# Chunked attention and a two-layer feed-forward block on one core: another planned order, copies of q on ScalarE, and weights of 14 groups turned by TensorE

## The chip, the core and the metric

The kernel runs on one core of a Trainium2 chip. The core has five engines, each with its own in-order list of instructions: TensorE (PE, matrix products into PSUM; its weight loads, PEld, overlap the products), VectorE (DVE), ScalarE (ACT), GpSimd (POOL) and SyncE (SP, which here only issues DMAs). They meet through semaphores. Sixteen DMA engines move data; a DMA is issued by an instruction on SP, on ScalarE or on GpSimd, and lands some microseconds later.

The metric is the device time of one execution in microseconds (us). The kernel before took 283.0, 283.0 and 281.61 us in three runs, median 283.0. The profile is of one more execution, which took 283.97 us; its span, from the first to the last instruction of the program, is 282.2 us.

## The reference

Attention inside chunks of 64 rows, over 8 batches, 8 heads and 576 rows (9 chunks), head size 64; then two matrix products with a leaky ReLU between them over the 4608 tokens.

```python
scores = scale * np.matmul(q_c, k_c.transpose(0, 1, 2, 4, 3))   # per chunk, 64 x 64
scores = scores - np.max(scores, axis=-1, keepdims=True)
attn = np.exp(scores)
attn = attn / (np.sum(attn, axis=-1, keepdims=True) + 1e-09)
out = np.matmul(attn, v_c)
...
x = np.ascontiguousarray(attn_out.transpose(0, 2, 1, 3)).reshape(B * S, H * D)   # 4608 x 512
h = x @ w_in                       # 512 x 2048
g = np.maximum(0.01 * h, h)
return (g @ w_out).astype(np.float32)   # 2048 x 512
```

## The kernel before

**Groups.** Attention runs over 36 groups u of 128 tokens (two chunks for each of eight heads). q, k and v are loaded from fp32 in DRAM to fp16 in SBUF by DMAs that GpSimd issues (`load_one`, L289, and `load_v`, L297); a group's q or k is one DMA, or two where it lies across two batches. v is kept for two batches at a time (`VB`), and one of them is loaded again when its last reader is done.

For each group q and k must be turned, so that the head size lies on the partitions. Either TensorE turns them (`turn`, L462: four transposes into PSUM, and a copy out), or a DMA issued by SP does (`turn_dma`, L483, into the tiles `QT` and `KT`). The sets `BY_PE` say which groups go which way; everything outside them goes by DMA. The turned q is then copied in two halves into `QZ`, one of three buffers whose other places are zeros (`spread_q`, L466), so that one product with 128 rows gives the scores of two heads (`scores`, L494). For groups turned by TensorE the copy reads PSUM and is VectorE's or ScalarE's; for the others it reads `QT` and is done by GpSimd (`COPY_P`, L252).

From the scores in PSUM on a chain follows: maximum (L503) and shift (L509) on VectorE, exp (L518) on ScalarE, sum (L524) on VectorE, the small addition of 1e-9 (`ze`, L530) on GpSimd from group 4 on, reciprocal (L536) and product (L548, the weights `en`) on VectorE. The weights are turned by TensorE (`turn_e`, L557, and a copy into `et`) for the groups in `BY_PE['e']`, by a DMA from SP otherwise (L570). `values` (L582) multiplies them with v into `xp`, and ScalarE writes `xT` (L592), a ring of twelve groups.

**The two layers** run over 14 blocks of tokens (four of 128, four of 256, six of 512). The first layer's unit is `mm1` (L683): 16 products of 128, 8 of 256 or 4 of 512 columns by block, evacuated by ScalarE with the leaky ReLU (L695). In blocks named in `L1S`, four units of eight 256-column products are replaced, for each entry, by a form with seven quarter products in place of eight (`layer1`, L888 for its products), with sums before and after on VectorE. The second layer is `mm2` (L706) in the first four blocks, and the same seven-product form (`product`, L784) in the others, with forms of the weights `WF` and of the activations (L757) made by VectorE.

**The order.** The kernel does not leave the order to a scheduler. Every piece of work is a task with the engines it may run on, an occupancy and a latency in microseconds, what it depends on, and a position. `Planner.run` plays a clock: at each step it takes, on the engine that is free first, the ready task with the lowest position, chooses the engine where there is a choice, and emits the instruction at once. So the order of every engine's list, and which engine does a copy, follow from the planner's numbers: the `copy` prices, `LAG`, the model of the DMA queues in `advance` and `run` (delays and landings by kind: sw for loads by GpSimd, turn for transpositions, hw for stores), and the hand-set `HOLD`, `NUDGE` and `TWEAK`. On the chip only the lists and the semaphores count: an engine waits at its next instruction until what that needs is there. A load on GpSimd also waits until the load eight before it has landed, which is mirrored in the planner:

```python
fl = self.flight.setdefault(t.dma[0] == "sw", [])
if len(fl) >= 8 and fl[-8] not in self.done:
    continue
```

PSUM has eight banks: six (`mm`) for products and turned q and k, one for the scores (`Sp`), one for turned weights and values (`ox`). `fill` (L1091) puts products of ones into planned gaps in the first 24 us.

Of the kernel before, what the change touches and what calls it, by code (L numbers as in the profile page):

```python
# [21 lines left out]
class Planner:  # L22
# [4 lines left out]
    def __init__(self, banks, slack, margin, hold, nudge):  # L27
# [5 lines left out]
        self.hold, self.nudge = hold, nudge  # L33
        self.slack, self.margin = slack, margin
# [24 lines left out]
    def advance(self, to):  # L59
# [12 lines left out]
    def finish(self, n, end):  # L72
        self.done[n] = end
        for key, left in list(self.held.items()):
            if n in left:
                left.discard(n)
                if not left:
                    del self.held[key]
                    self.banks[key[0]][key[1]] = end
        for m in self.after.get(n, ()):  # L80
            self.need[m] -= 1
            if self.need[m] == 0:
                self.can[m] = max([self.hold.get(m, 0.0)] + [self.done[d] + self.LAG for d in self.tasks[m].deps])

    def run(self):
# [8 lines left out]
        while self.can or self.landings or any(self.queues.values()):  # L94
            best = {}
            for n, since in self.can.items():
# [41 lines left out]
            if t.dma:  # L138
                kind, work, packet = t.dma
                ahead = min(6.0, sum(x[1] for x in self.queues.get("sw", ())))  # L140
                delay = {"sw": 1.35, "turn": ahead, "hw": 0.3 + ahead, "first": 1.2 + ahead}[kind]
                if kind == "sw" and not self.flight[True]:
                    delay = 2.2
# [8 lines left out]
def kernel(  # L152
# [24 lines left out]
    G = 2 * CH  # L177
# [6 lines left out]
    SUBS = {11:512,12:512}  # L184
    L1S = {8: (1,), 10: (1,), 11: (0, 1, 2), 12: (0, 1), 13: (0, 1, 2)}
    WQAT = 0.5
# [6 lines left out]
    ATT = -0.65  # L193
    FORM = -0.86
    WFAT = 0.31
    VLAG = 5
    BY_PE = {'q': (0, 1, 2, 3, 4, 5, 6, 7, 8, 13, 18), 'k': (0, 1, 2, 3, 4, 5, 6, 7, 8), 'e': (0, 1, 2, 3, 4, 5, 6, 7, 8, 19)}
# [4 lines left out]
    HOLD = {('v', 3): 28.7, ('k', 2): 14.1, ('q', 5, 0): 31.9, ('G', 0, 2, 0): 20.9, ('n', 0): 11.9, ('k', 3): 18.8, ('c', 0): 15.1, ('e', 0): 13.3, ('tq', 4): 24.6, ('s', 2): 15.0, ('G', 2, 2, 0): 33.8, ('q', 5, 1): 29.5, ('m', 1): 11.9, ('G', 2, 3, 0): 32.8, ('tq', 0): 6.1, ('tk', 5): 30.8, ('G', 2, 0, 0): 28.7, ('m', 4): 29.4}  # L202
    NUDGE = {('M', 12, 5, 0): 0.04, ('M', 8, 1, 1): 0.11, ('M', 13, 3, 0): 0.07, ('A', 9, 3, 1): -0.07, ('M', 11, 4, 0): -0.08}
    SPREAD = 1.26
    COPY_M = ("ACT", "DVE")
    COPY_L = ("ACT",)
    FILL = 24.0
    FILLS = 0.8
    MARGIN = 0.29
    TWEAK = {(4, 12): 0.39, (0, 4): -0.39, (5, 4): -0.05, (17, 5): -0.31, (32, 1): 0.26, (33, 5): -0.04, (4, 11): -0.13, (4, 2): -0.06, (0, 9): 0.13, (25, 2): -0.59, (2, 2): 0.3, (6, 0): 0.43}  # L210
    A_LEAD = 0.18
    ORDER = (1, 6, 5, 7, 2, 4, 3)
    ORDER1 = (1, 2, 6, 5, 7, 3, 4)
# [4 lines left out]
    def sub(j):  # L218
# [19 lines left out]
        {"mm": ["qp", "kp", "mm0", "mm1", "mm2", "mm3"], "Sp": ["Sp"], "ox": ["ox"]}, SLACK, MARGIN, HOLD, NUDGE  # L238
# [82 lines left out]
    RATE = {"row": 1 / 1120, "w": 1 / 188}  # L321

    def load(name, emit, deps, count, kind):
        issue = 0.58 + 0.00028 * count
        add(("landed",) + name, {"POOL": (issue, issue)}, emit, deps, pos=-20.0 + 0.001 * len(loads),
            dma=("sw", count * RATE[kind], RATE[kind]))
# [282 lines left out]
    for u in range(NU):  # L609
        p = att  # L610
        for n, name in enumerate("qk"):
# [6 lines left out]
            else:  # L618
# [4 lines left out]
                add(("t" + name, u), {"SP": (1.3, 1.3)}, turn_dma(name, u), here, dma=("turn", 0.9, 0.0014), pos=p(u, n))  # L623
        qe = {e: copy[e] for e in (COPY_Q if u in BY_PE["q"] else COPY_P)}
# [507 lines left out]
```

## Time and profile before

| what | value |
|---|---|
| three runs | 283.0, 283.0, 281.61 us |
| profiled execution | 283.97 us |
| its span | 282.2 us |
| TensorE busy, share of the span | 272.0 us, 96% |
| VectorE | 207.8 us, 74% |
| ScalarE | 174.0 us, 62% |
| GpSimd | 136.8 us, 48% |
| mean granted TensorE clock | 0.994 |
| read from HBM, written | 36.70 MB, 9.44 MB |

How to read it: busy time is the time in which an engine runs instructions of its own; a DMA that is under way is not in it. TensorE's products overlap, so a row's duration is longer than the step from one start to the next, and prices are taken start to start. In a timeline a row is a start, a duration, an engine, a line of the kernel, an operation, what is written and read, the shape and a count of merged instructions; a bracket tells the idle time ahead of it and what ended that. In busy time by stretches a row has the stretch's bounds and length, then busy time and number of instructions of PE, PEld, DVE, ACT and POOL, the granted TensorE clock, the DMA share and GB/s. In groups of instructions a row has the busy time and the mean duration of one in ns, then the idle time in front and what ended most of it. A row of the list of waits has the total, the number and the longest.

### The profile page before, as it was taken

To read this page: it belongs to the slowest core of one execution; us is meant where nothing else is said; L and a number is where in the kernel's file an instruction comes from. 1 tells how busy PE (TensorE), PEld (TensorE's weight loads), DVE (VectorE), ACT (ScalarE), POOL (GpSimd) and SP (SyncE) were. 2 spreads that over 40 slices of the span, in tenths; PEclk is the share of its full clock that TensorE was granted. 3 is DMA by queue.
4 is the path that set the end of the run, shared out by engine and by line. 5 is a ranking of instruction groups with operands and counts; after the bars stand their busy time and mean duration, and the time that the engine had idled before them with its cause. 6 is when DMAs were issued, how large, how long until landed. Compare 5 with 4: busy or idle time off the path is not lost.

```text
span 282.2 us, 7367 instructions
## 1 busy us (share of the span) xinstructions
PE 272.0 (96%) x3008; PEld 235.2 (83%) x3008; DVE 207.8 (74%) x365; ACT 174.0 (62%) x314; POOL 136.8 (48%) x194
## 2 busy tenths in 40 slices
PE   7799999996999999999999999999999999999995
PEld 7689965784899999999989899998788788888884
DVE  7698888474767768879837967889669977583752
ACT  5347765772656477776745566755787667877421
POOL 8858675837695545474946875565323000000000
PEclk9999999997999999999999999999999999999999
DMA  8999999999999999999999999999984113100223
GB/s 141 155 186 172 181 190 156 216 124 174 128 162 159 163 143 188 177 145 150 98 125 162 138 187 197 139 203 175 140 180 104 21 38 105 65 2 0 77 82 142
DMA packets 164193, 38.75 MB, mean 137 GB/s; under 512 B 155200, under 2 KB 159808, under 8 KB 164160
## 3 DMA queue, kind: packets, MB, share of 16 engines
q0 software_dynamic: 114336, 18.09, 95.4%
q1 hardware_dynamic: 48784, 19.93, 42.0%
q8 instruction: 23, 0.38, 0.6%
q10 hardware_dynamic: 1040, 0.26, 0.4%
q14 instruction: 10, 0.08, 0.1%
HBM read 36.70 MB, written 9.44 MB: 163 GB/s over the span
## 4 chain that ended last, share of the span: by engine, by line
PE 85%; DMA 8%; POOL 4%; issue 1%; DVE 0%; POOLq 0%
PE hT L683 30%; PE mb L784 20%; PE mc L784 10%; PE lb L888 6%; PE ma L784 5%; DMA q_in<-in_q_dram 5%; DMA k_in<-in_k_dram 4%; PE lc L888 3%; PE oP L706 3%; PE Sp L494 3%; PE xp L582 2%; PE la L888 2%; POOL q_in L289 1%; POOL w_inT L306 1%; POOL VB L297 1%
## 5 line engine op out<-in xcount | busy, mean ns | idle before, releaser
L683 PE MATMUL hT<-xT,w_inT 128*128 128x256 f16 (+2 forms) x912 | 103.2, 264 | 0.3
L683 PEld LDWEIGHTS <-w_inT 128*128 128x128 f16 x912 | 77.9, 98 | 11.6 <-issue 0.6
L695 ACT ACTIVATE gT<-hT 128x512 f16<-128x512 f32 x104 | 61.5, 596 | 42.1 <-PE hT L683 41.8
L784 PEld LDWEIGHTS <-gT 128*128 128x128 f16 x512 | 49.3, 98 | 6.0
L784 PEld LDWEIGHTS <-S 128*128 128x128 f16 x384 | 37.3, 99 | 4.9
L530 POOL TENSOR_SCALAR ze<-z 128x8 f32<-128x8 f32 x32 | 9.5, 298 | 61.5 <-DVE z L524 60.0
L252 POOL COPY QZ<-QT 64x512 f16<-64x512 f16 x50 | 34.2, 683 | 8.1 <-DMA QT<-q_in 5.3
L289 POOL DMA_DIRECT2D q_in<-in_q_dram x39 | 33.9, 870 | 8.5 <-DMA q_in<-in_q_dram 2.5
L289 POOL DMA_DIRECT2D k_in<-in_k_dram x39 | 33.5, 858 | 7.0 <-DVE et L250 1.7
L784 PE MATMUL mb<-WF,gT 128*128 128x256 f16 x256 | 33.2, 273 | 0.0
L784 PE MATMUL mc<-w_outT,S 128*128 128x256 f16 x256 | 33.2, 273 | 0.0
L524 DVE TENSOR_REDUCE z<-ex 128x8 f32<-128x512 f16 x36 | 24.5, 681 | 10.9 <-ACT ex L518 10.8
L503 DVE TENSOR_REDUCE mx<-Sp 128x8 f32<-128x512 f32 x36 | 24.5, 682 | 10.5 <-PE Sp L494 10.4
L592 ACT ACTIVATE xT<-xp 128x512 f16<-128x512 f32 x36 | 21.4, 595 | 11.2 <-PE xp L582 11.0
L548 DVE TENSOR_TENSOR en<-ex,zi 128x512 f16<-128x512 f16 x36 | 26.7, 741 | 0.3
L518 ACT ACTIVATE ex<-sh 128x512 f16<-128x512 f32 x36 | 22.6, 627 | 5.0 <-DVE sh L509 4.5
L509 DVE TENSOR_TENSOR sh<-Sp,mx 128x512 f32<-128x512 f32 x36 | 24.6, 683 | 0.4
L297 POOL DMA_DIRECT2D VB<-in_v_dram x16 | 18.7, 1171 | 7.0 <-PE xp L582 4.3
L494 PE MATMUL Sp<-KT,QZ 128*128 128x64 f16 x288 | 14.3, 193 | 3.5 <-POOL QZ L252 2.8
L784 PE MATMUL mb<-WF,S 128*128 128x256 f16 x128 | 17.5, 282 | 0.0
L494 PEld LDWEIGHTS <-QZ 128*128 128x128 f16 x288 | 12.8, 98 | 4.9 <-POOL QZ L252 2.9
L888 PEld LDWEIGHTS <-wq 128*128 128x128 f16 x160 | 15.0, 98 | 2.0
(82 smaller groups left out, 392.4 us busy)
## 6 DMA issues: line engine op xcount, KB each, us to landing
out_dram<-osb SPq DMA_DIRECT2D x10, 512.0 KB, 3.9
VB<-in_v_dram POOLq DMA_DIRECT2D x16, 288.0 KB, 9.4
q_in<-in_q_dram POOLq DMA_DIRECT2D x31, 128.0 KB, 10.6
k_in<-in_k_dram POOLq DMA_DIRECT2D x31, 128.0 KB, 10.2
out_dram<-osb SPq DMA_DIRECT2D x14, 256.0 KB, 6.1
w_inT<-in_moe_w_in_dram POOLq DMA_DIRECT2D x8, 256.0 KB, 7.6
w_outT<-in_moe_w_out_dram POOLq DMA_DIRECT2D x4, 512.0 KB, 10.8
q_in<-in_q_dram POOLq DMA_DIRECT2D x8, 64.0 KB, 8.1
```

Source lines behind the costliest of these rows:

```text
L252: nc.gpsimd.tensor_copy(out=out, in_=in_)
L289: nc.gpsimd.dma_start(out=qk[name, u][a - u * G:z - u * G], in_=SRC[name][a // S, :, a % S:a % S + z - a, :].rearrange("h p d -> p h d"),)
L494: nc.tensor.matmul(out=Sp[:, i, :], lhsT=qz[:, 2 * m + g, e, :, :], rhs=kt[:, 2 * m + g, e, :], start=True, stop=True)
L503: nc.vector.tensor_reduce(out=st["mx", u], in_=st["S", u], axis=AXL.X, op=ALU.max)
L509: nc.vector.tensor_tensor(out=st["sh", u], in0=st["S", u], in1=st["mx", u].unsqueeze(2).to_broadcast((128, 8, CH)), op=ALU.subtract,)
L518: nc.scalar.activation(out=st["ex", u], in_=st["sh", u], func=AFT.Exp, bias=0.0, scale=SCL)
L524: nc.vector.tensor_reduce(out=st["z", u], in_=st["ex", u], axis=AXL.X, op=ALU.add)
L548: (nc.vector if eng == "DVE" else nc.gpsimd).tensor_tensor(out=st["en", u], in0=st["ex", u], in1=st["zi", u].unsqueeze(2).to_broadcast((12 ...
L683: nc.tensor.matmul(out=hT[:, i, :], lhsT=w_inT[:, t, fc * 128:(fc + 1) * 128], rhs=xT[:, r0 % RING // G:(r0 % RING + tb) // G, t, :], star ...
L695: nc.scalar.activation(out=gT(j)[:, nf * a:nf * a + nf, h * tb:h * tb + tb], in_=HT.pop((j, a, h)), func=AFT.Prelu, bias=0.0, scale=1.0, a ...
L784: nc.tensor.matmul(out=to, lhsT=lhs[:, fc, p * 128:(p + 1) * 128], rhs=rhs[:, fc, :], start=(opens and (p == 0 or j == LAST) and fc == 0), ...
L888: nc.tensor.matmul(out=to[:, i, :], lhsT=lhs[:, t, i * 128:(i + 1) * 128], rhs=rhs[:, :, t, :], start=(m in OPENS and i == 0 and t == 0), ...
```

## The change

It has four parts.

1. The planner's DMA model gets other numbers: the delay from an issue to the start of its transfer, the time from the end of a transfer to its landing, the shares of transfers under way together, and the cap on the queue ahead. A load also waits, in the plan, `GUARD` after the landing of the load eight before it, and from 40 us on at most four loads are planned in flight (`DEPTH`, `DEEP`). The lists that come out differ on every engine.
2. `COPY_P` is ScalarE in place of GpSimd, with a planner's price of its own for copies that read SBUF (`copy_sb`).
3. `BY_PE` is changed: q for groups 0 to 9 (before 0 to 8, 13 and 18), k for 0 to 9 (before 0 to 8), weights for 0 to 11, 14 and 15 (before 0 to 8 and 19).
4. The rest: the seven-product form of the first layer on 11 units in place of 10, 512-column units in blocks 12 and 13 in place of 11 and 12, temporaries of the second layer's form copied by ScalarE alone, those of the first layer's by either, the last part of w_out loaded ahead of group 6, the banks `Sp` and `ox` given to products when attention is done, and the tuning numbers.

```diff
-                self.landings.append((to + {"sw": 1.5, "turn": 0.32 + self.margin, "hw": 0.65, "first": 1.3}[kind], n))
+                self.landings.append((to + {"sw": 1.0, "turn": 0.75 + self.margin, "hw": 0.05, "first": 1.35}[kind], n))
...
+        if n in self.gives:
+            self.banks["mm"][self.gives[n]] = end
...
-                    if len(fl) >= 8 and fl[-8] not in self.done:
-                        continue
+                    if len(fl) >= 8:
+                        if fl[-8] not in self.done:
+                            continue
+                        if t.dma[0] == "sw" and self.done[fl[-8]] > 24.0:
+                            since = max(since, self.done[fl[-8]] + self.guard)
+                    if t.dma[0] == "sw" and len(fl) >= self.depth and self.now > self.deep:
+                        if fl[-self.depth] not in self.done:
+                            continue
...
-                ahead = min(6.0, sum(x[1] for x in self.queues.get("sw", ())))
-                delay = {"sw": 1.35, "turn": ahead, "hw": 0.3 + ahead, "first": 1.2 + ahead}[kind]
+                ahead = min(3.6, sum(x[1] for x in self.queues.get("sw", ())))
+                delay = {"sw": 2.1, "turn": ahead, "hw": 1.23 + ahead, "first": 1.2 + ahead}[kind]
...
-    SUBS = {11:512,12:512}
-    L1S = {8: (1,), 10: (1,), 11: (0, 1, 2), 12: (0, 1), 13: (0, 1, 2)}
-    LEAD = 3.61
-    LOADS = 'Q0 g1 i v0.0 g2 v0.1 Q2 g3 Q1 g4 Q3 g5 P2 P0 g7 P1 g6 P3 v1.0 g8 v1.1'
+    SUBS = {12: 512, 13: 512}
+    L1S = {8: (1,), 9: (1,), 10: (0, 1), 11: (0, 1), 12: (0, 1), 13: (0, 1, 2)}
+    LEAD = 4.12
+    LOADS = 'Q0 g1 i v0.0 g2 v0.1 Q2 g3 Q1 g4 Q3 g5 P2 P0 g7 P1 P3 g6 v1.0 g8 v1.1'
...
-    COPY_P = ("POOL",)
+    COPY_P = ("ACT",)
...
-    BY_PE = {'q': (0, 1, 2, 3, 4, 5, 6, 7, 8, 13, 18), 'k': (0, 1, 2, 3, 4, 5, 6, 7, 8), 'e': (0, 1, 2, 3, 4, 5, 6, 7, 8, 19)}
+    BY_PE = {'q': (0, 1, 2, 3, 4, 5, 6, 7, 8, 9), 'k': (0, 1, 2, 3, 4, 5, 6, 7, 8, 9), 'e': (0, 1, 2, 3, 4, 5, 6, 7, 8, 9, 10, 11, 14, 15)}
...
+    GUARD = 0.84
+    DEPTH = 4
+    DEEP = 40.0
-    COPY_M = ("ACT", "DVE")
-    COPY_L = ("ACT",)
+    COPY_M = ("ACT",)
+    COPY_L = ("ACT", "DVE")
-    MARGIN = 0.29
+    MARGIN = 2.08
...
+    plan.gives = {("b", NU - 1): "Sp", ("a", NU - 1): "ox"}
...
+    copy_sb = {"DVE": (0.29, 0.33), "ACT": (0.60, 0.68), "POOL": (0.66, 0.70)}
...
-        qe = {e: copy[e] for e in (COPY_Q if u in BY_PE["q"] else COPY_P)}
+        qe = {e: copy[e] for e in COPY_Q} if u in BY_PE["q"] else {e: copy_sb[e] for e in COPY_P}
```

`HOLD` gains three entries (tq 2, G 1 0 0 and z 3), `NUDGE` and `TWEAK` have other entries, and the positions `ATT`, `FORM`, `WFAT`, `WQAT` and `SPREAD` and the order `ORDER1` other values. The built lists have 6034 rows on TensorE (before 6018, weight loads counted), 370 on VectorE (361), 327 on ScalarE (262), 129 on GpSimd (166) and 91 on SP (99), where equal neighbours share a row on all but the first.

More of the change, by code (lines that the diff above doesn't have):

```diff
@@ L25, with __init__ @@
     LAG = 0.06
-    def __init__(self, banks, slack, margin, hold, nudge):
+    def __init__(self, banks, slack, margin, hold, nudge, guard, late, depth, deep):
         self.tasks, self.done, self.began = {}, {}, {}
@@ L33, in __init__ @@
         self.hold, self.nudge = hold, nudge
+        self.guard, self.late = guard, late
+        self.depth, self.deep = depth, deep
+        self.gives = {}
         self.slack, self.margin = slack, margin
@@ L83, in finish @@
                 self.can[m] = max([self.hold.get(m, 0.0)] + [self.done[d] + self.LAG for d in self.tasks[m].deps])
+                if self.can[m] > 30.0:
+                    self.can[m] += self.late.get(m[0], 0.0)
     def run(self):
@@ L320 @@
     loads: list[tuple] = []
-    RATE = {"row": 1 / 1120, "w": 1 / 188}
+    RATE = {"row": 1 / 1120, "w": 1 / 193}
+    PACKET = {"row": 0.00102, "w": 0.00044}
     def load(name, emit, deps, count, kind):
@@ L325, in load @@
         add(("landed",) + name, {"POOL": (issue, issue)}, emit, deps, pos=-20.0 + 0.001 * len(loads),
-            dma=("sw", count * RATE[kind], RATE[kind]))
+            dma=("sw", count * RATE[kind], PACKET[kind]))
         loads.append(name)
```

39 lines of the change are left out of this document (20 added, 19 removed).

## The prediction

> **What bounds the kernel now.** I read the page first, then busy time by stretches, then TensorE's timeline around the one weak stretch, and only then the engine that TensorE waited for there.
>
> ```profile
> span 282.2 us, 7367 instructions
> PE 272.0 (96%) x3008; PEld 235.2 (83%) x3008; DVE 207.8 (74%) x365; ACT 174.0 (62%) x314; POOL 136.8 (48%) x194
> ...
> 0.00:22.00 22.00, 17.96 (x273) 16.23 (x274) 17.52 (x43) 10.54 (x16) 15.71 (x26) 1.00 1.63 162
> 22.00:62.00 40.00, 39.94 (x518) 31.55 (x516) 30.22 (x59) 27.08 (x48) 26.43 (x34) 1.00 1.87 174
> 62.00:72.00 10.00, 7.23 (x71) 5.84 (x69) 4.65 (x8) 3.81 (x8) 6.03 (x8) 0.83 1.75 167
> 72.00:212.00 140.00, 139.99 (x1526) 124.87 (x1524) 108.66 (x185) 91.76 (x168) 85.50 (x121) 1.00 1.77 158
> ```
>
> The columns of a stretch are its bounds and length, then busy time of PE, PEld, DVE, ACT and POOL, then TensorE's granted clock. From 22 to 62 and from 72 to 212 us TensorE is busy for 179.93 of 180 us at full clock: nothing but its own list of instructions sets the time there. Only two stretches hold time that is not work: the first 22 us, and 62 to 72, where 2.77 us are idle and the clock is 0.83. TensorE's timeline shows that hole (start, duration, what; the name behind the arrow ended the wait):
>
> ```profile
> 57.94 0.39 PE L557 MATMUL tpe<-ident,en 128*128 128x128 f16 x4
> 58.16 1.91 PE L683 MATMUL hT<-xT,w_inT 128*128 128x256 f16 x16
> 59.91 0.40 PE L582 MATMUL xp<-et,VB 128*128 128x64 f16 x8
> ...
> 62.11 1.04 PE L784 MATMUL mb<-w_outT,gT 128*128 128x256 f16 x8
> 62.98 0.40 PE L582 MATMUL xp<-et,VB 128*128 128x64 f16 x8
> 66.15 0.41 PE L494 MATMUL Sp<-KT,QZ 128*128 128x64 f16 x8 [2.77 <-POOL QZ L252]
> 66.39 2.65 PE L683 MATMUL hT<-xT,w_inT 128*128 128x256 f16 x16
> 68.83 1.92 PE L784 MATMUL mb<-WF,S 128*128 128x256 f16 x8
> 70.54 1.18 PE L683 MATMUL hT<-xT,w_inT 128*128 128x256 f16 x8
> 71.56 0.40 PE L494 MATMUL Sp<-KT,QZ 128*128 128x64 f16 x8
> ```
>
> Start to start gives the undisturbed prices: sixteen hT take 59.91 - 58.16 = 1.75, eight 256-column products 62.98 - 62.11 = 0.87, four transposes 58.16 - 57.94 = 0.22, eight 64-column ones 66.39 - 66.15 = 0.24. So the scores of group 9 should have begun at 62.98 + 0.24 = 63.22 and began 2.93 late. After it sixteen hT took 2.44 (0.69 too much), eight mb 1.71 (0.84), eight hT 1.02 (0.15): the half clock that followed the hole cost 1.68. **The stall is worth 4.61 us.** The chain behind it is GpSimd's:
>
> ```profile
> 46.51 0.88 POOL L289 DMA_DIRECT2D q_in<-in_q_dram  x1 [0.96 <-DMA VB<-in_v_dram]
> ...
> 51.40 0.87 POOL L289 DMA_DIRECT2D k_in<-in_k_dram  x1 [1.04 <-PE Sp L494]
> 52.39 2.30 POOL L297 DMA_DIRECT2D VB<-in_v_dram  x2
> ...
> 62.48 0.92 POOL L289 DMA_DIRECT2D q_in<-in_q_dram  x1 [2.47 <-DMA q_in<-in_q_dram]
> 63.93 0.88 POOL L289 DMA_DIRECT2D k_in<-in_k_dram  x1 [0.53 <-DMA k_in<-in_k_dram]
> 64.81 2.63 POOL L252 COPY QZ<-QT 64x512 f16<-64x512 f16 x4
> ```
>
> ```profile
> 51.53 1.35 SPq L483 DMA_TRANSPOSE QT<-q_in  x1
> 53.00 1.40 SPq L483 DMA_TRANSPOSE KT<-k_in  x1
> ...
> QT<-q_in SPq DMA_TRANSPOSE x1, 7.2
> KT<-k_in SPq DMA_TRANSPOSE x1, 9.4
> ```
>
> The last two rows are DMA issues, with the time to landing of those two. Group 9's turned q was there at 51.53 + 7.2 = 58.7 and its k at 53.00 + 9.4 = 62.4, before TensorE asked at 63.2. The two copies of q stood behind two load issues that each waited until an earlier load had landed, and ran from 64.81 to 66.1. So a queue position was late, not the data.
>
> **The change part by part.** *The stall, -4.61.* Group 9's q and k are now turned by TensorE, and its copies run on VectorE and ScalarE. From group 10 on ScalarE copies. No copy stands behind a load issue any more. What remains on GpSimd beside loads is the 32 small additions (ze), which still wait behind load issues; in the built order the additions of groups 8 and 9 stand behind both loads of group 12.
>
> *Copies on ScalarE, 0 on the path.* There are 52 in place of 50. The trace has no ScalarE copy between fp16 tiles in SBUF; the nearest rows bound it.
>
> ```profile
> L252 POOL COPY QZ<-QT 64x512 f16<-64x512 f16 x50 | 34.2, 683 | 8.1 <-DMA QT<-q_in 5.3 <-PE Sp L494 0.8
> L248 ACT ACTIVATE QZ<-qp 64x512 f16<-64x512 f16 x12 | 7.1, 592 | 7.3 <-PE qp L462 7.1
> L916 ACT ACTIVATE gT<-lu 128x512 f16<-128x512 f32 x10 | 6.3, 630 | 3.4 <-DVE lu L911 3.3
> ```
>
> The same shape out of PSUM takes 592 ns, a read of SBUF in fp32 630; I take 610: 52 x 0.61 = 31.7 us. ScalarE goes from 174 to about 206 us (73%), and in 72 to 212 from 91.8 to about 121 of 140 (86%). It hides under TensorE as long as no evacuation of PSUM is held up; if the cover is gone, each copy ahead of an evacuation costs up to its 0.61. Beside it the temporaries of the four-product blocks go to ScalarE alone (four VectorE evictions move there), and seven of the first layer's move to VectorE. I put 0 and keep 0 to 2 us.
>
> *TensorE's list, +0.45.* Weights are turned by TensorE for 14 groups instead of 10, k for 10 instead of 9, q for 10 instead of 11: net four more sets at 0.22, +0.88. The seven-product form of the first layer runs on 11 units instead of 10: 32 hT go (2 x 1.75 = 3.50), seven products of four come (28 x 0.87 / 8 = 3.05), -0.45. Exchanging which blocks use 512 columns keeps the columns. Filler matmuls go from 160 to 156, together 0.22 us at the 56 ns of a 128-column one (0.22 / 4); those before 21.6 us only fill waits. Added: 0.88 - 0.45 = 0.43, with rounding 0.45. VectorE gains 14 instructions net, under 10 us even if each were as long as a GpSimd copy (0.683), and has 207.8 of 282.2 in use: 0 while it keeps up.
>
> *First 22 us, 0.* TensorE gets under way when the k of group 3 lands:
>
> ```profile
> 20.83 0.44 PE L1098 MATMUL idle<-ones 128*128 128x128 f16 x5
> 21.64 0.40 PE L462 MATMUL kp<-ident,k_in 128*128 128x128 f16 x4 [0.37 <-DMA k_in<-in_k_dram]
> ```
>
> The loads up to it stand in the same order, and the same real products stand before this kp in both programs. So nothing is gained or lost; bounds: -0.65 (that filler and the 0.37 vanish) and +0.5 (it lands later). The fourth part of w_out is loaded before group 6's q and k instead of behind them; the products that need it come some two microseconds after it, and group 6's transposes about as late as before.
>
> *New small gaps, +0.5.* For groups 10, 11, 14 and 15 one 0.87 product stands between turning the weights and using them: 0.22 + 0.87 = 1.09 us for a transpose (0.39) and a copy, by these rows 0.42 or 0.59:
>
> ```profile
> L250 DVE COPY et<-tpe x7: 411/425/426, 15.9 to 129.0; 128x512 f16<-128x512 f16 x7
> L248 ACT ACTIVATE et<-tpe x3: 592/592/597, 37.6 to 48.4; 128x512 f16<-128x512 f16 x3
> ```
>
> That is 0.81 to 0.98, which just fits if the copying engine is free. One instruction of 0.6 ahead makes it 0.5 late: 0 to 2.0 for four groups; I take 0.5. The holes are too short to expect the half clock.
>
> On that half clock the Trainium skill, "TensorE: Matmul & The Clock Gate" (Part 1: The HAM clock gate), says that the clock falls to half after at least one idle window of about 3.4 us. Here 2.77 us of idle were enough; by the rule this hole would have cost 2.93 and the forecast below would be 1.68 higher, 281.0. The row decides.
>
> **The sum.** The profiled execution took 283.97 us, its span 282.2. 283.97 - 4.61 + 0.45 + 0 + 0 + 0.5 = 280.3. The runs shown are 283.0, 283.0 and 281.61; their median is 0.97 below the profiled one, so 280.3 - 0.97 = **279.3**. Its own range is 277.9 (first stretch -0.65, no gaps, and 0.3 of scatter) to 281.3 (gaps at 2).
>
> **The rivals.** *V too late (slower).* Adding the prices above along the built order from kp at 21.64, TensorE reaches the xp of group 9, the first that reads the reloaded V, at 67.3 now; before, 16 us of work lay between the scores and the xp of group 9, now 11.
>
> ```profile
> q_in<-in_q_dram POOLq DMA_DIRECT2D x1, 128.0 KB, 9.2
> ...
> k_in<-in_k_dram POOLq DMA_DIRECT2D x1, 128.0 KB, 12.2
> ...
> VB<-in_v_dram POOLq DMA_DIRECT2D x1, 288.0 KB, 18.5
> ```
>
> In before V's second half, issued at 53.53, landed at 53.53 + 18.5 = 72.0. If that holds, TensorE waits 4.7 us and pays the 1.68: 279.3 + 6.4 = 285.7. Against it: the loads queued between (q at 46.51 + 9.2 = 55.7, the last k at 51.40 + 12.2 = 63.6) now stand behind V, which frees 7.9 us of queue and puts V at 64. It costs anything from a landing after 67.3 and makes the kernel slower than before from 71.3. 0.06.
>
> *ScalarE's queue blocked (slower).* A copy that waits for its turned q now holds evacuations behind it.
>
> ```profile
> POOL QZ L252 <- DMA QT<-q_in: 5.3, 4, 3.2
> ...
> QT<-q_in SPq DMA_TRANSPOSE x25, 8.1
> ```
>
> Four such waits, the longest 3.2 us, cost nothing on GpSimd. On ScalarE TensorE can go on for as many units of 0.87 as it has free PSUM banks; with two of six free 1.7 us are covered, and a wait of 3.2 costs 1.5. Four of them make 279.3 + 6 = 285.3; slower than before beyond two and a half. The Trainium skill, "TensorE: Matmul & The Clock Gate" (table at the head), calls ScalarE's queue strictly first in, first out; no row here shows otherwise. For it: between issuing a q transposition and its copy lie only 7.3 to 7.9 us of TensorE work for groups 30, 34 and 35, under the median flight of 8.1. Against: for the other 23 groups it is 8 to 17 us, and those three would be late by 0.8 at most, which two free banks cover. 0.10.
>
> *Turned keys too late (about the same).* In the built order the least TensorE work between issuing a group's K transposition and its scores is 8.3 us (group 29; 8.6 and 8.8 for 30 and 33), before 9.0.
>
> ```profile
> DMA to landing us min/median/max: 2.5/7.8/9.4
> ```
>
> That is K's flight. At 9.4 these three and four more at 9.0 to 9.4 would be late by 0 to 1.1, together some 3: 282.3. For it: loads are now issued 14 to 27 us before the scores, before 22 to 38. Against: fewer loads queue at a time, and four transpositions go. 0.12.
>
> *The change does not do what it says:* the hole moves to the next wait on a ze addition behind load issues, at the same 4.6: 283.9 less what of it is hidden, say 283.0. 0.04.
>
> **How the numbers follow.** Forecast 0.68, the four rivals 0.06, 0.10, 0.12 and 0.04. A measurement cannot tell less than about 0.5%, 1.4 us, from no change: faster is below 281.6, slower above 284.4. Faster: 0.66 of the forecast, 0.05 of late keys with small delays, 0.03 of the blocked queue with one wait: 0.74. Slower: 0.05 of V, 0.05 of the queue, 0.03 of keys and the moved hole: 0.13. The rest, 0.13, is the same. The range runs from 277.9 to 284.3 and leaves the slow ends out.
>
> **What would show it.** Right: no idle time of TensorE over 1 us after 22 us, clock 1.00 in 62 to 72, TensorE's last product about 4 us earlier, ScalarE near 206 us and GpSimd near 100. Copies between 590 and 640 ns. Wrong: a hole before xp of group 9 ended by VB; ScalarE rows QZ whose idle time was ended by a QT landing, with TensorE waiting for an evacuation; holes before Sp ended by KT around groups 29 to 33; or half clock anywhere after 10 us.

## The result, and the profile after

| | before | after |
|---|---|---|
| median of 20 runs each | 282.85 us (281.42 to 288.42) | 279.66 us (278.59 to 283.32) |
| ratio | | 0.9904, 95% interval [0.9876, 0.9931] |
| profiled execution, span | 283.97, 282.2 | 280.69, 278.6 |
| last product starts | 278.59 | 275.25 |

A ratio leaves out, on both sides, the runs more than 1.5% above the fastest of the same kernel, and 21 of the 23 runs of before that the experiments below lose in this way have the half clock, so medians of all runs stand beside the ratios.

The forecast was 279.3, the range 277.9 to 284.3. The page after, busy time by engine:

```profile
span 278.6 us, 7389 instructions
...
PE 270.7 (97%) x3016; PEld 234.7 (84%) x3016; DVE 209.8 (75%) x379; ACT 199.9 (72%) x365; POOL 101.9 (37%) x144
```

Busy time by stretches, after:

```profile
0.00:22.00 22.00, 18.52 (x280) 16.79 (x281) 17.62 (x43) 10.87 (x17) 16.17 (x26) 1.00 1.61 162
22.00:62.00 40.00, 39.43 (x512) 30.83 (x510) 32.34 (x65) 26.48 (x49) 23.29 (x30) 1.00 1.83 177
62.00:72.00 10.00, 10.00 (x116) 9.08 (x114) 5.94 (x11) 9.00 (x18) 4.65 (x6) 1.00 1.85 122
72.00:212.00 140.00, 139.20 (x1536) 125.71 (x1534) 112.04 (x199) 114.38 (x211) 57.07 (x79) 1.00 1.78 151
```

The stretch from 62 to 72 went from 7.23 busy at a clock of 0.83 to 10.00 at 1.00. GpSimd's 85.50 in the long stretch fell to 57.07 and ScalarE's 91.76 rose to 114.38. The waits and the places where they stand, TensorE's list of waits first, then its timeline:

```profile
PE qp L483 <- DMA q_in<-in_q_dram: 0.9, 2, 0.5
PE Sp L515 <- ACT QZ L268: 0.8, 1, 0.8
PE xp L603 <- DMA et<-en: 0.8, 1, 0.8
```

```profile
21.11 0.38 PE L483 MATMUL kp<-ident,k_in 128*128 128x128 f16 x4
...
67.81 0.40 PE L603 MATMUL xp<-et,VB 128*128 128x64 f16 x8
68.05 0.40 PE L515 MATMUL Sp<-KT,QZ 128*128 128x64 f16 x8
...
199.66 0.60 PE L909 MATMUL lb<-xT,wq 128*128 128x256 f16 x4
201.07 0.39 PE L603 MATMUL xp<-et,VB 128*128 128x64 f16 x8 [0.80 <-DMA et<-en]
```

The wait for `QZ` is of the first 10 us, with two that are left out (1.3 for `ones`, 0.2 for `k_in`). After 22 us nothing over 1 us is left. Start to start, against the median step of the same form, four spots are late (a place is the start of the last product ahead of the late one): 0.25 at 39.55, 0.19 at 48.92, 0.62 at 51.33 (q of group 9 had not landed) and 0.96 at 199.99 (weights of group 28, turned by a DMA that took 11.3 us): 2.02 us together. That DMA was issued between 185 and 192 us, beside a store of 512 KB, where the two loads of 128 KB took 17.3 and 18.6 us. The xp of group 9, at 67.81, did not wait for V. The copies, and the DMA flights from 30 to 215 us (size and median to landing), after:

```profile
L268 ACT ACTIVATE QZ<-QT 64x512 f16<-64x512 f16 x52 | 32.5, 624 | 0.7
```

```profile
q_in<-in_q_dram POOLq DMA_DIRECT2D x26, 128.0 KB, 7.4
...
QT<-q_in SPq DMA_TRANSPOSE x26, 6.6
```

and the same view of before:

```profile
q_in<-in_q_dram POOLq DMA_DIRECT2D x25, 128.0 KB, 10.9
...
QT<-q_in SPq DMA_TRANSPOSE x25, 8.1
```

The median load lands in two thirds of the time and the median transposition 1.5 us sooner; k goes the same way. ScalarE stood idle for 0.7 us in all ahead of these copies: none was held by a late turned q to any effect.

### The profile page after: what moved, and what is told of

Its sections match the earlier page's. It is cut to its first block, busy times and chain, and to the rows that moved or that the text cites. A ratio compares the mean times of both kernels' runs of the same rounds, so it can differ in the third digit from the quotient of the medians.

```text
span 278.6 us, 7389 instructions
## 1 busy us (share of the span) xinstructions
PE 270.7 (97%) x3016; PEld 234.7 (84%) x3016; DVE 209.8 (75%) x379; ACT 199.9 (72%) x365; POOL 101.9 (37%) x144
## 4 chain that ended last, share of the span: by engine, by line
PE 76%; DMA 18%; POOL 3%; issue 1%; DVE 0%; POOLq 0%
PE hT L704 25%; PE mb L805 19%; PE mc L805 9%; DMA q_in<-in_q_dram 7%; PE lb L909 6%; PE ma L805 5%; DMA w_outT<-in_moe_w_out_dram 4%; DMA et<-en 4%; PE lc L909 3%; DMA w_inT<-in_moe_w_in_dram 3%; PE xp L603 3%; PE Sp L515 2%; PE la L909 2%; POOL k_in L309 1%; POOL q_in L309 1%
## 5 line engine op out<-in xcount | busy, mean ns | idle before, releaser
L704 PE MATMUL hT<-xT,w_inT 128*128 128x256 f16 (+2 forms) x880 | 99.3, 263 | 0.2
L704 PEld LDWEIGHTS <-w_inT 128*128 128x128 f16 x880 | 74.8, 98 | 10.8 <-DMA w_inT<-in_moe_w_in_dram 0.3
L716 ACT ACTIVATE gT<-hT 128x512 f16<-128x512 f32 x100 | 58.0, 594 | 23.2 <-PE hT L704 22.7
L551 POOL TENSOR_SCALAR ze<-z 128x8 f32<-128x8 f32 x32 | 7.8, 242 | 99.7 <-DVE z L545 98.6
L268 ACT ACTIVATE QZ<-QT 64x512 f16<-64x512 f16 x52 | 32.5, 624 | 0.7
L569 DVE TENSOR_TENSOR en<-ex,zi 128x512 f16<-128x512 f16 x36 | 24.5, 683 | 0.3
L909 PEld LDWEIGHTS <-wq 128*128 128x128 f16 x176 | 16.6, 98 | 2.0
L805 PE MATMUL mb<-w_outT,gT 128*128 128x256 f16 x128 | 16.6, 273 | 0.0
L805 PE MATMUL mb<-WF,S 128*128 128x256 f16 x128 | 16.6, 273 | 0.0
L805 PE MATMUL ma<-w_outT,gT 128*128 128x256 f16 x128 | 16.6, 273 | 0.0
```

Source lines behind the costliest of these rows:

```text
L268: nc.scalar.activation(out=out, in_=in_, func=AFT.Copy, bias=0.0, scale=1.0)
L569: (nc.vector if eng == "DVE" else nc.gpsimd).tensor_tensor(out=st["en", u], in0=st["ex", u], in1=st["zi", u].unsqueeze(2).to_broadcast((12 ...
L704: nc.tensor.matmul(out=hT[:, i, :], lhsT=w_inT[:, t, fc * 128:(fc + 1) * 128], rhs=xT[:, r0 % RING // G:(r0 % RING + tb) // G, t, :], star ...
L716: nc.scalar.activation(out=gT(j)[:, nf * a:nf * a + nf, h * tb:h * tb + tb], in_=HT.pop((j, a, h)), func=AFT.Prelu, bias=0.0, scale=1.0, a ...
L805: nc.tensor.matmul(out=to, lhsT=lhs[:, fc, p * 128:(p + 1) * 128], rhs=rhs[:, fc, :], start=(opens and (p == 0 or j == LAST) and fc == 0), ...
L909: nc.tensor.matmul(out=to[:, i, :], lhsT=lhs[:, t, i * 128:(i + 1) * 128], rhs=rhs[:, :, t, :], start=(m in OPENS and i == 0 and t == 0), ...
```

## The experiments

All of them compute the whole reference. In the table the gaps are the sum of TensorE's late starts of more than 0.15 us after 22 us in the one profile, worked out start to start as above; "before beside it" is the median of all runs of the kernel before on the same chip (29, 35 or 29 runs; 20 in the row of after).

| kernel | gaps | last product starts | median (runs) | before beside it | ratio |
|---|---|---|---|---|---|
| before | 3.3, and 1.7 of half clock | 278.59 | | | |
| before, second profile | 3.0, and 1.7 of half clock | 278.16 | 283.54 (1) | 283.33 | |
| after | 2.0 | 275.25 | 279.66 (20) | 282.85 | 0.9904 [0.9876, 0.9931] |
| two loads behind the copies | 3.1 | 277.67 | 282.01 (12) | 282.51 | 1.0004 [0.9969, 1.0038] |
| hole filled | 1.1 beside the filled one | 278.62 | 283.82 (12) | 282.51 | 1.0055 [1.0020, 1.0091] |
| copies moved, order kept | 7.2 | 280.26 | 285.95 (6) | 282.51 | 1.0145 [1.0098, 1.0192] |
| copies moved and planned | 4.0 | 277.43 | 283.20 (12) | 283.33 | 0.9967 [0.9921, 1.0012] |
| DMA model alone | 5.8 | 279.09 | 284.72 (12) | 283.62 | 1.0081 [1.0048, 1.0115] |
| parts 1 to 3 | 4.1 | 278.45 | 283.59 (12) | 283.33 | 1.0054 [1.0023, 1.0086] |
| after, copies on GpSimd | 3.8 | 277.18 | 283.23 (12) | 282.51 | 1.0048 [1.0013, 1.0082] |
| after, old DMA model | 1.3 | 274.85 | 281.91 (12) | 283.62 | 0.9936 [0.9898, 0.9975] |
| after, fewer weights by TensorE | 3.6 | 275.98 | 281.71 (12) | 283.62 | 0.9962 [0.9926, 0.9999] |
| after, second profile | 0.15 | 273.41 | 280.87 (12) | 283.62 | 0.9949 [0.9911, 0.9986] |
| after, three more seven-product units | 5.9 | 279.15 | 285.15 (12) | 283.33 | 1.0074 [1.0030, 1.0118] |

### Was it the queue position, and did the hole bring the half clock?

**Two loads behind the copies** (before, GpSimd's loads of group 14 emitted after the copies of group 9's q):

```diff
-            t.emit(e, tag, at)
+            late = (("landed", "q", 14, 0), ("landed", "k", 14, 0))
+            if n not in late:
+                t.emit(e, tag, at)
+            if n == ("q", 9, 1):
+                for x in late:
+                    self.tasks[x].emit("POOL", None, at)
```

> The kernel before, with one thing moved: on GpSimd the loads of group 14's q and k stand behind the two copies of group 9's q instead of ahead of them; all other lists are unchanged. Queue position (my theory): group 9's q is turned at 58.7 and its k at 62.4 us, so the copies run at about 60 to 61.3, the scores of group 9 start at 63.2 without a hole, no half clock follows, span 282.2 - 4.6 = 277.6, time about 278.4 (0.984 of the kernel before). Data late (rival): the hole stays, ratio 1.00. Hole moves (rival): a hole of the same kind opens at the copies of group 10 or at the delayed loads of group 14, ratio 0.99 to 1.00.

TensorE's timeline of this kernel:

```profile
64.84 0.40 PE L562 MATMUL tpe<-ident,en 128*128 128x128 f16 x4 [1.12 <-DVE en L553]
65.08 1.04 PE L789 MATMUL mb<-w_outT,gT 128*128 128x256 f16 x8
65.95 0.40 PE L587 MATMUL xp<-et,VB 128*128 128x64 f16 x8
66.19 0.40 PE L499 MATMUL Sp<-KT,QZ 128*128 128x64 f16 x8
```

The scores follow their xp by 0.24, with no wait: the queue position was what held them. But a small addition (ze) of an earlier group still stands behind a load issue, as GpSimd's timeline shows:

```profile
62.60 0.68 POOL L294 DMA_DIRECT2D k_in<-in_k_dram  x1 [2.28 <-DMA k_in<-in_k_dram]
63.35 0.23 POOL L535 TENSOR_SCALAR ze<-z 128x8 f32<-128x8 f32 x1
```

The weights `en` come late with it, and a hole of 1.29 opens 1.4 us earlier in the list; another of 0.61 comes at 130.87. All 12 runs have a mean clock of 0.999 or more, but the median of all runs falls by 0.50 only, and the ratio is 1.0004 where 0.984 was expected. The place of the stall is confirmed; that its removal alone is worth 4.61 is not. The rival of a hole that moves fits better, though this hole stands at another place than it named.

**The hole filled** (before, 48 products of ones ahead of group 9's scores):

```diff
+            if u == 9:
+                idle = psum([128, 4, 128], FP32, "idle", tag)
+                for i in range(48):
+                    nc.tensor.matmul(out=idle[:, i % 4, :], lhsT=ones, rhs=ones, start=True, stop=True)
```

> The kernel before, with 48 products of ones (128 columns, 56 ns each, 2.7 us) put into TensorE's list ahead of the scores of group 9, into the bank of the scores. Theory that the half clock is the hole's second price (1.68 us): the scores start as late as before (within 0.1), the clock stays at 1.00 in 62 to 72, and the time falls by 1.7 us, ratio 0.994. Rival, that the clock falls for another reason or that the hole alone counts: clock 0.83 again, ratio 1.00.

Its timeline:

```profile
63.97 2.84 PE L493 MATMUL idle<-ones 128*128 128x128 f16 x48
67.83 0.41 PE L498 MATMUL Sp<-KT,QZ 128*128 128x64 f16 x8 [1.01 <-POOL QZ L252]
68.07 1.91 PE L687 MATMUL hT<-xT,w_inT 128*128 128x256 f16 x16
69.82 1.04 PE L788 MATMUL mb<-WF,S 128*128 128x256 f16 x8
```

Here the scores came 67.83 - 63.97 = 3.86 after the place where the list had reached them, and yet sixteen hT take 1.75: with the hole filled but for 1.01, no half clock, and 0.998 or more in all 12 runs. Beside it 11 of the 29 runs of before have 0.994 or less. So the half clock follows the hole. The expected ratio of 0.994 did not come (1.0055). The 48 products take 48 x 0.056 = 2.69. Where the hole is longer they are free; where it is shorter they cost the rest. The median rose to 283.82, and the 18 runs of before on this chip with a clock of 0.998 or more have a median of 282.05. By these two numbers the hole of a run without the half clock is about 2.69 - 1.77 = 0.9 us: a rough estimate, since no profile of before shows such a run, and it takes all else in these two sets of runs for equal, of which one is chosen by its clock and the other is not.

**Before, unchanged, profiled again:**

> The kernel before, unchanged, profiled a second time. Theory: landings differ from execution to execution, so the hole at 63 us is of another size here: under 1.5 us and without the half clock in 62 to 72 if this execution takes 282.6 or less, with it if it takes 283.7 or more. Rival: the hole is a fixed property of the order, 2.8 +- 0.3 us with a clock near 0.83 in that stretch again, and the spread of the times comes from elsewhere.

```profile
63.48 0.40 PE L582 MATMUL xp<-et,VB 128*128 128x64 f16 x8
65.89 0.41 PE L494 MATMUL Sp<-KT,QZ 128*128 128x64 f16 x8 [2.01 <-POOL QZ L252]
66.14 3.55 PE L683 MATMUL hT<-xT,w_inT 128*128 128x256 f16 x16
69.48 1.11 PE L784 MATMUL mb<-WF,S 128*128 128x256 f16 x8
```

The hole is 2.18 late start to start (2.01 idle) instead of 2.94, and sixteen hT took 69.48 - 66.14 = 3.34 in place of 1.75. The time, 283.54, lies between the theory's two cases; the half clock is as the rival had it, the hole is below its 2.5. What stands is that the hole varies: 2.94, 2.18 and, in the filled kernel, 3.86. Over three chips 41 of 93 runs of before have a mean clock of 0.994 or less, and their median is 2.3, 1.6 and 3.0 us above that of the others on the same chip; of the changed kernel's 32 runs one does, and of the 114 runs of the other versions nine, four of them in the version with three more seven-product units.

### Which part carries the gain?

**Copies moved, order kept** (before's order, the 50 copies emitted on ScalarE):

```diff
-            t.emit(e, tag, at)
+            t.emit("ACT" if n[0] == "q" and e == "POOL" else e, tag, at)
```

> The kernel before, with the same planned order; the 50 copies of q that GpSimd did are issued on ScalarE at the same place of the plan. Queue position: the copies no longer stand behind loads, the hole at 63 us goes, span about 277.6, ratio 0.984, ScalarE about 205 us busy; where ScalarE is dense its evacuations come up to 1.2 us later, which six banks cover. Rival, ScalarE's queue blocked: copies that wait for turned q (four waits on GpSimd before, 3.2 us the longest) hold evacuations, TensorE waits for them, ratio 1.00 to 1.01.

Its list of TensorE's waits:

```profile
PE Sp L494 <- ACT QZ L248: 2.6, 4, 1.0
PE lb L888 <- ACT lu L248: 1.8, 2, 1.6
...
PE xp L582 <- DMA et<-en: 1.1, 1, 1.1
```

The hole at 63 is gone, and 7.2 us of gaps come in its place: copies that ScalarE reaches late, and an evacuation (`lu`) behind a copy. So with the cover gone the kernel is 1.45% slower, though the hole is gone too.

**Copies moved and planned** (before, part 2 of the change alone: `COPY_P` and `copy_sb`, the order planned with that price):

> The kernel before with part 2 of the change alone, planned: COPY_P is ScalarE and the planner has the price of copies that read SBUF; DMA model, BY_PE and tuning are those of before. Theory (moving the copies pays as soon as the plan prices them): no TensorE gap over 1 us at 60 to 72, the 5.1 us of gaps of the unplanned move shrink below 2, ratio to before 0.995 to 1.000. Rival (the copies need the model that the order is planned with as well, or the tuning): gaps of 3 us or more in 72 to 212 that ScalarE ends, ratio 1.005 to 1.015.

The median of all runs is the same as before's within 0.13 us. The 7.2 us of gaps shrink to 4.0; the largest are 1.25 at 131.68 (weights turned by a DMA), 0.85 at 226.80 and 0.73 at 61.41. The price in the plan removes 3.2 us of the gaps of the unplanned move, but they do not shrink below 2 as the theory had it, and the part alone brings nothing that shows.

**The DMA model alone** (before, planned with the new numbers of part 1, `MARGIN` and the cap on loads in flight; copies stay on GpSimd):

```diff
-                delay = {"sw": 1.35, "turn": ahead, "hw": 0.3 + ahead, "first": 1.2 + ahead}[kind]
+                delay = {"sw": 2.1, "turn": ahead, "hw": 1.23 + ahead, "first": 1.2 + ahead}[kind]
...
-    MARGIN = 0.29
+    MARGIN = 2.08
```

> The kernel before, planned anew with the fitted DMA model of the change (delays, landings, packet shares, guard, depth, margin); copies stay on GpSimd, and BY_PE and the tuning numbers stay. If the model alone brings the gain (rival), the hole at 63 us is gone, clock 1.00 in all executions, ratio 0.99. If copies on GpSimd still stand behind loads (my theory after the exchange of engines above cost 3.5 us), waits of Sp for GpSimd's QZ remain, 2 to 4 us in sum, ratio 0.998 to 1.01.

```profile
PE mb L791 <- ACT tu L254: 2.3, 2, 1.8
...
PE hT L690 <- ACT xT L599: 0.9, 1, 0.9
```

No half clock in 12 runs and no hole at 63, but 5.8 us of gaps from 80 to 136: 4.75 ended by evacuations of ScalarE, 1.05 by VectorE, none by a DMA. Waits of the scores for GpSimd's copies, which the theory expected, did not come. The model alone makes the kernel slower, although the flights are shorter: the loads of 128 KB have medians of 6.0 and 6.7 us, before 10.9.

**Parts 1 to 3** (after without part 4, that is with the tuning numbers, the blocks of the seven-product form, the copy engines of the temporaries, the load order and the bank rule of before):

```diff
-    L1S = {8: (1,), 9: (1,), 10: (0, 1), 11: (0, 1), 12: (0, 1), 13: (0, 1, 2)}
-    LEAD = 4.12
+    L1S = {8: (1,), 10: (1,), 11: (0, 1, 2), 12: (0, 1), 13: (0, 1, 2)}
+    LEAD = 3.61
...
-    plan.gives = {("b", NU - 1): "Sp", ("a", NU - 1): "ox"}
```

> The changed kernel without part 4: DMA model, copies on ScalarE and BY_PE are those of after, tuning numbers, blocks of the seven-product form, order of the last w_out load and the two given banks are those of before. Theory (the first three parts carry the gain when they go together): TensorE's list is 0.45 longer than that of after, gaps after 22 us under 2, ratio to before 0.990 to 0.996. Rival (the hand-set numbers, found for one model, carry it): gaps of 3 us or more after 22 us, or a start later by 1 us, ratio 1.000 to 1.010.

By stretches:

```profile
72.00:212.00 140.00, 139.99 (x1526) 124.92 (x1524) 107.05 (x189) 113.13 (x204) 57.16 (x78) 1.00 1.79 160
...
212.00:230.00 18.00, 15.42 (x155) 11.75 (x153) 15.25 (x25) 12.42 (x24) 1.57 (x3) 1.00 0.17 36
```

The three parts together keep TensorE's list unbroken from 22 to 212, and 3.9 us are lost between 212 and 228, where the last groups of attention are under way (their last scores start at 222.1); k of an early group also landed late, with a wait of 1.3 at 15 us. In the changed kernel 212 to 230 is 18.00 of 18. So part 4 carries the end, as the rival's numbers have it. That it is the hand-set numbers, as the rival says, is not shown, since part 4 is more than these. The two given banks come too late for most of the loss: `Sp` is free with the last shift, at 226.0. The units of block 11 are another candidate. The four versions with three of them and the copies on ScalarE, this one among them, have gaps of 1.3 to 5.6 us from 205 to 230; the four with two of them and the copies there have 0.17 or less; with three and the copies on GpSimd it is 0.18 or less. No run changes block 11 alone.

**After, copies on GpSimd** (after's order):

```diff
-            t.emit(e, tag, at)
+            t.emit("POOL" if n[0] == "q" and n[1] > 9 else e, tag, at)
```

> The changed kernel, with the same planned order; the 52 copies from turned q in SBUF are issued on GpSimd at the same place of the plan. If the move to ScalarE is what removed the stall, copies stand behind loads that wait for a landing again, and holes of 1 to 4 us before scores come back, ratio to the kernel before 0.995 to 1.01. If the order planned with the fitted queue model is enough by itself (rival), loads no longer block for long, and the time stays as in the changed kernel, ratio 0.99.

```profile
PE Sp L515 <- POOL QZ L272: 2.7, 3, 1.0
```

Three holes of 0.88, 1.19 and 1.10 at 67, 130 and 162, and the whole gain is lost: the new order needs the copies off GpSimd. The order of before, planned with them there, had no such hole from 72 to 212.

**After, unchanged, and two of its parts undone:**

Unchanged:

> The changed kernel again, unchanged, as the yardstick for the runs beside it and for a second profile. Ratio 0.990 within 0.003. If stalls come from DMA landings that differ from one execution to the next (what the four runs before suggest: the mean granted clock of the kernel before is 0.992 to 0.994 in 11 of 29 executions and 0.998 or more in the others), its holes of 0.2 to 1.0 us after 22 us stand at other places than in the first profile, together 1 to 3 us. If they are fixed by the order (rival), the same holes come back at tq of group 9 and at the xp of group 28.

With the old DMA model:

> The changed kernel, planned anew with the DMA model of the kernel before (delays, landings, packet shares, margin, no guard, no depth). If the fitted model is a needed part, TensorE waits more for landings (QT, KT, et, VB, q_in), in sum 2 to 5 us more than in the changed kernel, ratio 0.997 to 1.01. If ScalarE's copies with their own price are what counts (rival), ratio 0.990 as the changed kernel.

With fewer weights turned by TensorE:

> The changed kernel, planned anew with weights turned by TensorE for groups 0 to 8 alone; groups 9, 10, 11, 14 and 15 go by DMA. TensorE's list is 5 x 0.22 = 1.1 us shorter. If those five only relieve nothing (rival), ratio 0.986. If they shield the values from late landings, as their early place suggests, TensorE waits 1 to 4 us more before xp or Sp in 65 to 110 us: ratio 0.990 to 1.00. My guess is 0.993.

The edits of the last two, in this order:

```diff
-                delay = {"sw": 2.1, "turn": ahead, "hw": 1.23 + ahead, "first": 1.2 + ahead}[kind]
+                delay = {"sw": 1.35, "turn": ahead, "hw": 0.3 + ahead, "first": 1.2 + ahead}[kind]
...
-    GUARD = 0.84
-    DEPTH = 4
+    GUARD = 0.0
+    DEPTH = 8
```

```diff
-    BY_PE = {..., 'e': (0, 1, 2, 3, 4, 5, 6, 7, 8, 9, 10, 11, 14, 15)}
+    BY_PE = {..., 'e': (0, 1, 2, 3, 4, 5, 6, 7, 8)}
```

The changed kernel in its second profile, by stretches:

```profile
72.00:212.00 140.00, 140.00 (x1551) 126.63 (x1549) 112.88 (x199) 114.05 (x210) 56.53 (x79) 1.00 1.77 155
```

Its list is unbroken there; the two larger holes of the first profile did not come back, and that execution took 278.86. It is the fastest of the 12, whose median is 280.87, so its 0.15 us of gaps are not typical: the expected 1 to 3 us would fit the median. The ratio, 0.9949, lies outside the expected 0.990 within 0.003; the medians of all runs have 280.87 / 283.62 = 0.9903. With the old DMA model the flights are long again:

```profile
q_in<-in_q_dram POOLq DMA_DIRECT2D x26, 128.0 KB, 13.0
...
QT<-q_in SPq DMA_TRANSPOSE x26, 8.0
```

Its profile is nearly as good (1.3 us of gaps) and its median 1.04 longer, but its ratio of 0.9936 is no worse than 0.9949, and the intervals overlap. Four of those 12 runs are at 284.6 or more, where none of the unchanged kernel's 12 passes 283.0. With fewer weights turned by TensorE the list is five sets of 0.22 shorter and 3.6 us of gaps come, most of them between 94 and 132 in front of ScalarE's evacuations:

```profile
PE mb L805 <- ACT tu L268: 0.7, 2, 0.4
PE mb L805 <- ACT tw L268: 0.7, 1, 0.7
```

Both intervals overlap that of the changed kernel, so neither part can be given a price of its own.

### A version beyond it

**Three more units of the seven-product form:**

```diff
-    L1S = {8: (1,), 9: (1,), 10: (0, 1), 11: (0, 1), 12: (0, 1), 13: (0, 1, 2)}
+    L1S = {8: (1,), 9: (0, 1), 10: (0, 1), 11: (0, 1, 2), 12: (0, 1, 2), 13: (0, 1, 2)}
```

> The changed kernel with the seven-product form of the first layer on 14 units in place of 11 (one more in blocks 9, 11 and 12). Theory (TensorE's list is the only bound, each such unit is worth 0.45): three units give -1.35 us, ratio to before about 0.4 to 0.5 points below that of the changed kernel on the same footing, 0.985 to 0.990, with no gap over 0.5 us in 72 to 212. Rival (VectorE, at 112 to 113 of 140 us there, holds the units up, each adding three sums of 0.69 and its forms): VectorE above 119 of 140 and TensorE's gaps ended by VectorE of more than 1.4 us in sum, ratio 0.992 or more.

TensorE's timeline of this kernel, the rows with a wait between 212 and 227:

```profile
213.05 0.60 PE L909 MATMUL lb<-xT,wq 128*128 128x256 f16 x4 [0.70 <-ACT lw L268]
215.50 0.41 PE L515 MATMUL Sp<-KT,QZ 128*128 128x64 f16 x8 [0.58 <-ACT QZ L268]
218.01 1.05 PE L805 MATMUL mb<-WF,S 128*128 128x256 f16 x8 [1.43 <-DVE S L778]
220.85 1.91 PE L805 MATMUL mb<-WF,gT 128*128 128x256 f16 x16 [0.68 <-ACT tu L268]
...
226.04 1.03 PE L805 MATMUL mc<-w_outT,S 128*128 128x256 f16 x8 [0.45 <-ACT osb L268]
```

The list is 1.35 shorter by the price of a unit, and the kernel is slower than before. From 72 to 212 the theory holds (139.89 of 140, VectorE at 115.7, under the rival's 119); the loss is at 212 to 227, the same place as in the kernel of parts 1 to 3, which also has three units in block 11, and five of the six waits there (the one left out is 0.45 for `tw`) are for ScalarE. The sixth and longest, 1.43, is for VectorE, as much as the rival asked for, though not in the stretch whose load it had in mind. By the median of all runs no version tried beats the changed kernel.

## Why the prediction was right

**The stall, -4.61.** Right in place and mechanism for the profiled execution: its 62 to 72 us now hold 10.00 of work at full clock. What stayed unseen is that 4.61 is a price of executions like that one. The hole varies with the landings, the half clock comes in 41 of 93 runs, and by the rough estimate above a run without it has a hole of perhaps 0.9. And the price is that of the whole new order: taken away by itself, the stall passed to the next wait, as the fourth rival had it for the change.

**The sum against the median.** For the profiled execution the sum had 280.3, and 280.69 was measured. Subtracting 0.97, the distance of the profiled execution from the median, took some of that excess out again. The changed kernel's profiled execution stands 280.69 - 279.66 = 1.03 above its median too, but for another reason, its 2.02 us of gaps at full clock. The two offsets agree by chance, and part of the closeness of 279.3 to 279.66 is due to that. The prediction's own upper end, 281.3, needs the first stretch at +0.5 beside the gaps at 2 that it names; those alone give 280.8.

**TensorE's list, +0.45.** After the kp of group 3 the list has 14 products of 128 columns more and 4 of 256 columns fewer: 14 x 0.056 - 4 x 0.109 = 0.35. The 0.10 that is missing from the forecast are the two filler products of before behind this kp, which the prediction left out of its sum. The last product starts 3.34 earlier. Counting every step, late starts after that kp fell from 5.20 to 2.05, 3.15 less; the kp itself starts 0.53 earlier (21.11 for 21.64); 3.15 + 0.53 - 0.35 = 3.33.

**First 22 us, 0.** Mis-sized: -0.53, inside its bounds; k of group 3 landed at 20.5 instead of 21.6. In the second profile that kp starts at 21.15.

**New gaps, +0.5.** Mis-sized and misplaced: 2.02 in the profiled execution, 0.15 in the second. Late starts beside the stall were 5.20 - 4.61 = 0.59 before, so the term measured 2.05 - 0.59 = +1.46 in the profiled execution. None is at groups 10, 11, 14 or 15, whose weights TensorE turns; the largest is a transposition by DMA for group 28, then q of group 9, a load. These vary like the old hole.

**Copies, 0 on the path.** 624 ns against 610, 32.5 us against 31.7, ScalarE 199.9 against about 206 (some of the rest is that the first layer's evacuations of `hT` fell from 104 to 100). That they cost nothing holds for this plan: in the order that does not know of them the kernel was 1.45% slower.

**The rivals.** V's second half landed at 62.5, near the 64 worked out, and the xp did not wait. The landing of 71.3 from which V would have made the kernel slower does not come out of the sums beside it: 67.3 + (283.0 - 279.3) = 71.0, or 69.3 where the wait costs the 1.68 of half clock as well. No blocked queue: 0.7 us idle before all 52 copies. No late key: the median flight of k fell from 7.8 to 6.4, and though one issued at 191.15 took 11.6, no scores waited for a key.

**What made the gain.** The parts that were tried alone do not bring it: copies alone 0.9967 with an interval that holds 1, model alone 1.0081. Nor do parts 1 to 3 together, 1.0054, or the new order with the old engine, 1.0048. Parts 3 and 4 were not tried alone; in particular no run turns q and k of group 9 by TensorE in the order of before, which by itself would take the stalled copies off GpSimd. The kernel is at 96 to 97% of TensorE, so a part can only remove gaps, and most orders that differ in one part have gaps of 3.6 to 7.2 us elsewhere (1.3 with the old DMA model). That tuning their numbers anew would close these was not tried. How much of the 3.19 us is the half clock, how much the hole without it and how much other waits, was not settled: it would need a profile of before without the half clock. The runs give a hint: where both kernels ran side by side with their clocks, the medians are 2.75 apart (283.62 and 280.87), and the 17 runs of before without the half clock have 282.55, still 1.68 above.

## What to carry to other kernels

A stall read from one profile has that execution's price; look at the granted clock of many runs before it goes into a sum, and expect the next wait in the same queue to take part of it over. When an order is planned by prices, moving work to another engine has to be judged with the order planned anew for it: the same move had 7.2 us of gaps in the old order and 4.0 in a new one. That the tuning belongs to it as well is likely from the kernel of parts 1 to 3, but not shown. Part 1, which plans with at most four loads in flight, shortened the median flights of loads and transpositions, and that alone brought no time, since TensorE then waited for evacuations. The cap by itself was not tested.

## What the hardware showed beside this

**VectorE is slower beside GpSimd's copies.** The product of weights took 741 ns before and 683 after. The rows below are of before, of before's order with the copies on ScalarE, of after, and of after's order with the copies on GpSimd:

```profile
L548 DVE TENSOR_TENSOR en<-ex,zi 128x512 f16<-128x512 f16 x36 | 26.7, 741 | 0.3
```

```profile
L548 DVE TENSOR_TENSOR en<-ex,zi 128x512 f16<-128x512 f16 x36 | 24.7, 685 | 0.3
```

```profile
L569 DVE TENSOR_TENSOR en<-ex,zi 128x512 f16<-128x512 f16 x36 | 24.5, 683 | 0.3
```

```profile
L569 DVE TENSOR_TENSOR en<-ex,zi 128x512 f16<-128x512 f16 x36 | 26.9, 750 | 0.3
```

So 56 to 67 ns of each product go with the copies, in both orders. Over all 14 profiles the product takes 724 to 751 ns where GpSimd copies, and 683 to 685 where it does not. The Trainium skill, "SBUF — State Buffer" (Who interferes with whom), says that a VectorE instruction with two SBUF inputs contends with a GpSimd instruction that reads SBUF, and one that has at most one, outside the two-port modes, does not. The trace agrees: the shift, which reads the scores from PSUM, took 683 ns before and 686 after.

**The half clock came after 2.01 us of idle time**, shorter than the 2.77 of the first profile, and well below the window of about 3.4 us that the Trainium skill, "TensorE: Matmul & The Clock Gate" (Part 1), gives. In other profiles holes of 1.80 (the DMA model alone) and 1.63 (copies moved, order kept) were followed by full clock. The record of the clock shows a grid. In both profiles of before the half clock came 61.44 us after the clock's first rise (at 5.96 and 4.76) and lasted 3.413 us (67.40 to 70.82 in the first, 66.20 to 69.61 in the second), and 61.44 is 18 x 3.413. It came after the scores had started again, at 66.15 and 65.89. In the 3.413 us ahead of it TensorE was idle for 2.16 and 2.01 us; in no other stretch of this grid, over all 14 profiles up to 275 us, was it idle for more than 1.80. The first profile's hole of 2.77 began 0.61 us ahead of its stretch. So where a hole lies on the grid may decide beside its length, which would help to explain why only some runs pay; no run tests it. One stretch at half clock lowers the mean clock of 282 us by 3.413 / 2 / 282 = 0.006, which gives the 0.994 of the first profile.

**Flights are shorter in the orders planned with part 1.** In every profile of such an order, which plans at most four loads in flight, the 128 KB loads have medians of 6.0 to 8.1 us, in every other one 10.9 to 13.4; the transpositions of q and k, 6.0 to 7.2 against 7.5 to 8.6, move with them though SP issues them. Part 1 changes more numbers than this cap, so the depth as the cause is likely and not shown.
